# An mlp1 product of 64 rows issued inside the row-max visits (mixed attention and mlp kernel)

## The chip, the cores and the metric

The kernel runs on one core of one Trainium2 chip. The metric is the device time of one execution in microseconds; 1118.32 us is the median of 3 runs of the kernel before (1118.24 to 1118.5).

## What is computed

All inputs are float32. For 2048 tokens x of width 448, with 16 heads of 28 numbers and an mlp of width 1792:

```python
def _A_ref(x, wqkv, wo):
    qkv = transpose((x @ wqkv).reshape(B, S, 3, H, Dh), 2, 0, 3, 1, 4)
    q, k, v = qkv[0], qkv[1], qkv[2]
    scores = jnp.einsum("bhqd,bhkd->bhqk", q, k) * (Dh ** -0.5)
    p = _softmax(scores, axis=-1)
    o = jnp.einsum("bhqk,bhkd->bhqd", p, v)
    return transpose(o, 0, 2, 1, 3).reshape(B, S, D) @ wo

def _B_ref(x, w1, b1, w2, b2):
    y = _layernorm(x, axis=-1)
    h = _gelu(jnp.einsum("bsd,df->bsf", y, w1) + b1)
    return jnp.einsum("bsf,fd->bsd", h, w2) + b2

x = A_x
g = _sigmoid((x * gate_w).sum(-1, keepdims=True))
return g * _A_ref(x, A_wqkv, A_wo) + (1 - g) * _B_ref(x, B_w1, B_b1, B_w2, B_b2)
```

## The kernel before

**Precision.** Matrix products run in float32r. To come near float32 an operand is split in a high and a low part, and a product is made of three: high by high, high by low, low by high.

**Stages.** First q, k, v and the layernorm's statistics (L157 to L341); then the mlp (L599 to L668); then attention, four groups of four heads, with the output projection in the last group. In all stages TensorE (PE) has one hand-written order of instructions.

**The mlp** takes the tokens in NC = 4 groups `c` of 512. For each group, 14 calls of `mlp1(c, f)` (L564) make 128 of the 1792 hidden features each, and then four calls of `mlp2(c, i)` (L579) make 128 tokens' output each. The contraction of mlp1 is 448 = 3 x 128 + 64 long. Its first three parts take three products each. For the last 64 rows the launch code stores the weights twice, in rows 0 to 63 and 64 to 127, and `ln_low` (L140) puts the high part of y in rows 0 to 63 and the low part in rows 64 to 127 of `yh[:, 3]`. So two products of 128 rows do for them: `w1h[f][:, 3]` by `yh[:, 3]` is high by high plus high by low, and `w1l[f][:, 3]` by `yh[:, 3]` is low by high, plus low by low, which isn't needed. That makes 11 products of 128x128 weights by 512 columns in a call (L572), all added up in PSUM bank 0 or 1 (`f % 2`). Two ScalarE gelus read the bank (L575, L576). A call of mlp2 makes 42 products of 448 columns (L585, L586, L590).

**Row maxima beside it.** The softmax needs the maximum of each row of scores. `RowMax` (L343) computes, ahead of attention, scores of q by k from the high parts alone and reduces them. Its work is cut in groups `n` of 4 heads and 512 queries. In a group, 64 products of 28 contraction rows (L402) are to be made: 16 for each head `j`, whose rows lie at `32 * j`, so that head 0 has strip 0 (rows 0 to 27), head 1 strip 1 and so on. A 65th step, `close` (L366), transposes the finished maxima (L368) in the next group's time. `issue(first, n, rows)` (L374) makes `n` such products in PSUM banks `first`, `first + 1`, ...; it takes each from the head with the most left, or from the heads in `rows`, and falls back on the head with the most left if those have none. VectorE reduces the banks, two neighbouring ones in one instruction (L384) where the columns of their results ascend, and one alone otherwise (L382).

**When.** `Filler` (L426) spreads 482 of the row-max steps (MLP_MAX) evenly over the mlp stage. After each mlp1 product the code calls `filler.run` with that product's slot, 0.233 (W1; 0.65 of it in the first group of tokens), and in mlp2 with 0.205 (W2) or twice that. When at least MG = 6 steps are due, `run` makes one **visit**: `issue(2, 6)`, six steps in banks 2 to 7. The rest of the row maxima is made in the attention stage. When a group is nearly done, `issue` loads the next queries (L410), and near the end of a group of heads it has the keys of the next one loaded by `load_khr` (L460), a quarter of the keys at a time, once all four heads have used it (L413).

Of the kernel before, what the change touches and what calls it, by code (L numbers as in the profile page):

```python
# [32 lines left out]
MG = 6  # L33
FS = 4
W1, W2 = 0.233, 0.205
# [6 lines left out]
def kernel(ctx: ExitStack, tc: tile.TileContext, xt, wqk, wv, wo, xk, w1, b1, w2, b2,  # L42
                          ident_d, sel_d, out):
    nc = tc.nc
# [38 lines left out]
    w1h, w1l, w2h, w2l = {}, {}, {}, {}  # L83
# [36 lines left out]
    yh, yl = (my.tile([P, n, CH], F32R, name=f"y{n}") for n in (4, 3))  # L120
# [222 lines left out]
    class RowMax:  # L343
# [29 lines left out]

        def issue(self, first, n, rows=None):  # L374

            held = []

            def reduce():
                if held:
                    (b0, c0), (b1, c1) = held[0], held[-1]  # L380
                    if b0 == b1:
                        nc.vector.reduce_max(self.mx[:, c0:c0 + 1], bank[:, b0], axis=AX)  # L382
                    else:
                        nc.vector.reduce_max(self.mx[:, c0:c1 + 1:c1 - c0], bank[:, b0:b1 + 1], axis=AX)  # L384
                    held.clear()

            for b in range(first, first + n):
                if self.done >= NG * NC * 65:
                    break
                self.done += 1  # L390
                left = sum(len(x) for x in self.left)
                if self.last is not None and (left <= 56 or self.n == NG * NC):
                    reduce()
                    self.close(bank[:, b])
                    continue
                most = max(range(4), key=lambda j: (len(self.left[j]), -j))
                j = max(rows, key=lambda j: len(self.left[j])) if rows else most
                if not self.left[j]:
                    j = most
                i, k = self.left[j].pop(0)  # L400
                r = slice(32 * j, 32 * j + DH)
                nc.tensor.matmul(bank[:, b], self.qds[self.n][r, i * P:(i + 1) * P],  # L402
                                 khi[self.n // NC][r, k * 512:(k + 1) * 512], start=True, stop=True)
                at = (j * TPC + i) * 4 + k
                if held and held[0][1] > at:
                    reduce()
                held.append((b, at))
                if len(held) == 2:
                    reduce()
                if left == 41 and self.n + 1 < NG * NC:  # L410
                    self.load(self.n + 1)
                g, c = divmod(self.n, NC)
                if c == NC - 1 and g < MLP_G and all(n != k for x in self.left for _, n in x):  # L413
                    load_khr(g + 1, k)
                if left == 1:
                    reduce()
                    self.last = mpool.tile([P, 4 * TPC], F32, name="mf")
                    nc.vector.reduce_max(self.last, self.mx.rearrange("p (a k) -> p a k", k=4), axis=AX)
                    if self.n + 1 < NG * NC:
                        self.begin(self.n + 1)  # L420
                    else:
                        self.n += 1
                        self.left = [[]] * 4
            reduce()

    class Filler:  # L426
# [19 lines left out]
            left = self.upto - self.done  # L446
            return left if self.slot >= self.slots else min(left, int(due))

        def run(self, n=1):


            if self.max is not None and self.due(n) >= min(MG, self.upto - self.done) > 0:
                self.max.issue(2, min(MG, self.upto - self.done))

    filler = Filler()

# [3 lines left out]
    def load_khr(g, k=None, queue=nc.sync):  # L460

        sl = slice(0, S) if k is None else slice(k * CH, (k + 1) * CH)
        for j in range(4):
            r = D + (4 * g + j) * DH
            queue.dma_start(khr[32 * j:32 * j + DH, sl].bitcast(F32), qk[0, r:r + DH, sl])
# [98 lines left out]
    def mlp1(c, f):  # L564

        ps = bank[:, f % 2]
        ops = []
        for t in range(3):
            ops += [(w1h[f][:, t], yh[:, t]), (w1h[f][:, t], yl[:, t]), (w1l[f][:, t], yh[:, t])]
        ops += [(w1h[f][:, 3], yh[:, 3]), (w1l[f][:, 3], yh[:, 3])]  # L570
        for i, (a, b) in enumerate(ops):
            nc.tensor.matmul(ps, a, b, start=(i == 0), stop=(i == len(ops) - 1))  # L572
            filler.run(W1 if c else 0.65 * W1)
        h = mh.tile([P, CH], F32, name="h", bufs=2)
        nc.scalar.activation(hh[f], ps, AF.Gelu_apprx_tanh, bias=b1s[:, f:f + 1])  # L575
        nc.scalar.activation(h, ps, AF.Gelu_apprx_tanh, bias=b1s[:, f:f + 1])  # L576
        nc.gpsimd.tensor_sub(hl[f], h, hh[f].bitcast(F32))  # L577
# [21 lines left out]
    with texts:  # L599
# [12 lines left out]
        for c in range(NC):  # L612
            for f in range(NF):
                if c == 0:
                    if f == 0:
                        stages += [lnr[:, 0], lnr[:, 1]]
                        filler.max = RowMax()
                    for k in stage(f - 1):
                        low(k)
                    for k in order[3 * f // 2:3 * (f + 1) // 2]:  # L620
                        fetch_w2(k) if k < NF else fetch_w1(k - NF, staged())
                    for k in stage(f):
                        high(k)
                    if f == 1:
                        load_khr(0, queue=nc.gpsimd)
                    if f == FS:
                        filler.spread(nc.sync, MLP_MAX, 11 * W1 * (0.65 * (NF - FS) + 3 * NF) + W2 * (3 * NF * (NT - 1) - 24))
                mlp1(c, f)
            if c == 0:
                rest = order[3 * (NF - 1) // 2 - 1:]  # L630
# [5 lines left out]
            if c == NC - 1:  # L636
# [3 lines left out]
                first = {3: aq.tile([P, S], F32, name="klo", bufs=2), 2: aq.tile([P, NT, P], F32, name="vg", bufs=2)}  # L640
# [152 lines left out]
    with tc.manual_schedule(engines=ENGINES):  # L793
# [7 lines left out]
        while u < 4 * steps:  # L801
# [4 lines left out]
            while at < units[-1] // 4:  # L806
                at += 1
                n, k = divmod(at, NT)
                g, c = divmod(n, NC)
# [47 lines left out]
            if ended:  # L857
                n = summed // NT - 1
# [62 lines left out]
```

## Time and profile before

| | us |
|---|---|
| median of 3 runs | 1118.32 (1118.24 to 1118.5) |
| the profiled execution | 1119.32 |
| its span, first to last instruction | 1117.5 |
| mlp stage within it, about | 117 to 467 |
| VectorE pair reductions (L384), 203, mean of one | 1.22 |
| VectorE single reductions (L382), 618, mean of one | 0.69 |

How to read the profile: PE is TensorE's products, PEld its weight loads, which can run beside products; DVE is VectorE, ACT ScalarE, POOL GpSimd, SP the engine that issues most DMAs. A row of the timeline has the start, the length, the engine, the line of the kernel, the operation, the tiles written and read, the shapes (28*128 is 28 contraction rows by 128 weight columns) and how many instructions are merged in it; in brackets stands how long the engine was idle before, and what ended the wait. The ends of PE's products are modelled, and a product's row is longer than its share of a stream, so prices are taken from differences of starts. Row names such as `y` and `w1f` leave buffer numbers out.

### The profile page before, as it was taken

How to read it: one execution, taken by the hardware profiler on the slowest of the kernel's cores; microseconds unless marked ns; L12 is line 12 of the kernel's file. 1: busy time of each engine (PE TensorE's matmuls, PEld its weight loads, DVE VectorE, ACT ScalarE, POOL GpSimd, SP SyncE). 2: the span in 40 equal slices, each digit the busy share in tenths (PEclk: the TensorE clock that was granted, in tenths of full speed). 3: DMA queues.
4: the chain of work that ended last, by engine and by line, in shares of the span. 5: the costliest groups of instructions: out<-in, count | busy, mean ns of one | idle time of the engine just before them, and what ended most of it. 6: DMA issues, size and time to landing. Idle time of an engine off the chain costs nothing.

```text
span 1117.5 us, 19782 instructions
## 1 busy us (share of the span) xinstructions
PE 1105.8 (99%) x8136; PEld 672.7 (60%) x8136; DVE 738.9 (66%) x1029; ACT 634.4 (57%) x662; POOL 333.4 (30%) x354
## 2 busy tenths in 40 slices
PE   7999999999999999999999999999999999999998
PEld 5888777777777777744444444444444444454546
DVE  3534398988889889576766766676667767746103
ACT  5324551230241132288787877887877878847572
POOL 4006665343334331013113221320223024342350
PEclk9999999999999999999999999999999999999999
DMA  8988541011120113163100220012021003002111
GB/s 263 302 273 309 170 135 58 9 47 36 50 55 32 30 43 96 38 157 89 28 18 19 61 69 22 22 28 52 26 60 36 18 20 94 12 26 70 55 32 58
DMA packets 53079, 84.35 MB, mean 75 GB/s; under 512 B 8516, under 2 KB 28500, under 8 KB 52076
## 3 DMA queue, kind: packets, MB, share of 16 engines
q1 hardware_dynamic: 48732, 76.27, 22.7%
q0 software_dynamic: 4256, 6.81, 2.5%
q8 instruction: 64, 1.05, 0.4%
q14 instruction: 27, 0.22, 0.1%
HBM read 56.40 MB, written 26.49 MB: 74 GB/s over the span
## 4 chain that ended last, share of the span: by engine, by line
PE 96%; DMA 2%; DVE 1%; ACT 1%; POOL 0%; SPq 0%; issue 0%
PE bank L788 22%; PE bank L525 20%; PE bank L402 16%; PE bank L572 13%; PE bank L207 5%; PE bank L590 5%; PE bank L585 4%; PE bank L586 4%; PE bank L223 3%; PE bank L693 1%; PE bank L694 1%; PE bank L695 1%; DMA raw<-in_xt 1%; DMA raw<-in_wqk 1%; DMA raw<-in_wv 0%; DMA s<-in_w 0%
## 5 line engine op out<-in xcount | busy, mean ns | idle before, releaser
L529 ACT ACTIVATE pt<-bank 128x1536 f32<-128x1536 f32 (+1 forms) x387 | 461.9, 1244 | 141.0 <-PE bank L525 140.8
L382 DVE TENSOR_REDUCE mx<-bank 128x1 f32<-128x512 f32 x618 | 409.6, 687 | 173.1 <-PE bank L402 159.1
L788 PE MATMUL bank<-pt,vg 128*32 128x512 f32 x1950 | 261.6, 602 | 0.0
L384 DVE TENSOR_REDUCE mx<-bank 128x2 f32<-128x1024 f32 x203 | 238.9, 1219 | 29.2 <-PE bank L402 28.8
L402 PE MATMUL bank<-khi,qd 28*128 28x512 f32 x512 | 241.7, 479 | 0.1
L402 PEld LDWEIGHTS bank<-khi,qd 28*128 28x128 f32 x512 | 92.3, 181 | 148.1 <-DVE mx L382 106.9
L525 PE MATMUL bank<-qh,klo 28*128 28x512 f32 x1024 | 174.7, 393 | 0.0
L525 PE MATMUL bank<-qh,khi 29*128 29x512 f32 x768 | 157.2, 480 | 0.0
L572 PE MATMUL bank<-y,w1f 128*128 128x512 f32 x616 | 152.4, 398 | 1.1 <-ACT h L576 1.1
L572 PEld LDWEIGHTS bank<-y,w1f 128*128 128x128 f32 x616 | 112.5, 188 | 34.8 <-issue 10.9
L525 PE MATMUL bank<-ql,khi 28*128 28x512 f32 x768 | 129.6, 390 | 0.0
L577 POOL TENSOR_TENSOR hl<-h,hh 128x512 fp32r<-128x512 f32 x56 | 73.7, 1317 | 117.5 <-ACT h L576 77.3
L788 PEld LDWEIGHTS bank<-pt,vg 128*32 128x32 f32 x1950 | 44.6, 108 | 77.2 <-issue 76.7
L525 PEld LDWEIGHTS bank<-qh,klo 28*128 28x128 f32 x1024 | 87.6, 185 | 4.0
L575 ACT ACTIVATE hh<-bank,b1s 128x512 fp32r<-128x512 f32 x56 | 38.5, 687 | 90.3 <-PE bank L572 90.3
L709 POOL DMA_DIRECT2D lt<-ob x15 | 10.9, 725 | 250.9 <-DVE ob L708 250.9
L596 ACT ACTIVATE h<-bank 128x448 f32<-128x448 f32 x16 | 8.7, 545 | 134.5 <-PE bank L590 100.2
L590 PE MATMUL bank<-w2h,hl 128*128 128x448 f32 x224 | 85.0, 379 | 0.0
L525 PEld LDWEIGHTS bank<-qh,khi 29*128 29x128 f32 x768 | 60.8, 181 | 39.6 <-ACT pt L529 26.7
L585 PE MATMUL bank<-w2h,hh 128*128 128x448 f32 x224 | 83.3, 372 | 0.0
L586 PE MATMUL bank<-w2l,hh 128*128 128x448 f32 x224 | 81.9, 365 | 0.0
L402 PE MATMUL bank<-khr,qd 28*128 28x512 f32 x512 | 80.1, 467 | 0.2 <-DVE mx L384 0.2
(122 smaller groups left out, 1294.6 us busy)
## 6 DMA issues: line engine op xcount, KB each, us to landing
qk<-hl SPq DMA_DIRECT2D x28, 512.0 KB
raw<-in_xt SPq DMA_DIRECT2D x16, 256.0 KB
vs<-vt SPq DMA_DIRECT2D x16, 256.0 KB
s<-in_xt SPq DMA_DIRECT2D x16, 256.0 KB
rc<-rls POOLq DMA_DIRECT2D x60, 64.0 KB, 2.2
bxr<-in_xk SPq DMA_DIRECT2D x8, 448.0 KB
gbs<-h SPq DMA_DIRECT2D x16, 224.0 KB
klo<-qk SPq DMA_DIRECT2D x16, 224.0 KB
```

The lines of the kernel that those rows point to most:

```text
L207: nc.tensor.matmul(ps, a, b, start=(i == 0), stop=(i == len(ops) - 1))
L382: nc.vector.reduce_max(self.mx[:, c0:c0 + 1], bank[:, b0], axis=AX)
L384: nc.vector.reduce_max(self.mx[:, c0:c1 + 1:c1 - c0], bank[:, b0:b1 + 1], axis=AX)
L402: nc.tensor.matmul(bank[:, b], self.qds[self.n][r, i * P:(i + 1) * P], khi[self.n // NC][r, k * 512:(k + 1) * 512], start=True, stop=True)
L525: nc.tensor.matmul(bank[:, p], a[r, k * P:(k + 1) * P], b[r], start=(i == 0), stop=(i == 2))
L529: nc.scalar.activation(t, bank[:, at[0]:at[-1] + 1], AF.Exp, scale=SCALE)
L572: nc.tensor.matmul(ps, a, b, start=(i == 0), stop=(i == len(ops) - 1))
L577: nc.gpsimd.tensor_sub(hl[f], h, hh[f].bitcast(F32))
L585: nc.tensor.matmul(a, hh[f][:, sl], w2h[f], start=(f == 0), stop=False)
L586: nc.tensor.matmul(a, hh[f][:, sl], w2l[f], start=False, stop=False)
L590: nc.tensor.matmul(a, hl[f][:, sl], w2h[f], start=False, stop=(f == NF - 1))
L788: nc.tensor.matmul(pv[32 * j:32 * j + 32, :], vg[n // NC][:, k, 32 * j:32 * j + 32], probs.pop(4 * step + j), start=(k == 0), stop=(k == N ...
```

## The change

`mlp1` asks `filler.visits` whether a visit falls behind one of the first nine of the call's eleven slots. If so, the eleventh product, `w1l[f][:, 3]` by `yh[:, 3]`, is left out of the list, and its rows 0 to 63 alone (low by high, without low by low) are issued as a product of their own at the start of the first visit in the call, into the call's own bank. The six steps of that visit take their heads in a fixed order: 2, 3, 0, 1, 2, 3. The tenth product then closes the sum, and the eleventh slot is still counted. Without such a visit the call stays as it was.

```diff
@@ issue
-                j = max(rows, key=lambda j: len(self.left[j])) if rows else most
+                of = rows[b - first] if rows and isinstance(rows[0], list) else rows
+                j = max(of, key=lambda j: len(self.left[j])) if of else most
                 if not self.left[j]:
                     j = most
@@ Filler
-        def run(self, n=1):
+        def run(self, n=1, half=None):
             if self.max is not None and self.due(n) >= min(MG, self.upto - self.done) > 0:
-                self.max.issue(2, min(MG, self.upto - self.done))
+                m = min(MG, self.upto - self.done)
+                if half is None or m < MG:
+                    self.max.issue(2, m)
+                    return False
+                first, product = half
+                product()
+                side = [2, 3] if first == 0 else [0, 1]
+                self.max.issue(2, m, [[side[0]], [side[1]]] + [[j] for j in range(4)])
+                return True
+            return False
+
+        def visits(self, slots):
+            if self.max is None:
+                return 0
+            slot, done, n = self.slot, self.done, 0
+            for x in slots:
+                slot += x
+                due = self.first + (self.upto - self.first) * min(1, slot / self.slots) - done
+                if slot < self.slots and min(self.upto - done, int(due)) >= MG:
+                    done += MG
+                    n += 1
+            return n
@@ mlp1
-        for i, (a, b) in enumerate(ops):
-            nc.tensor.matmul(ps, a, b, start=(i == 0), stop=(i == len(ops) - 1))
-            filler.run(W1 if c else 0.65 * W1)
+        slot = W1 if c else 0.65 * W1
+        alone = filler.visits([slot] * 9) == 0
+        rest = lambda: nc.tensor.matmul(ps, w1l[f][:64, 3], yh[:64, 3], start=False, stop=False)
+        for i, (a, b) in enumerate(ops if alone else ops[:-1]):
+            nc.tensor.matmul(ps, a, b, start=(i == 0), stop=(i == len(ops) - (1 if alone else 2)))
+            if filler.run(slot, None if alone or rest is None else (0, rest)):
+                rest = None
+        if not alone:
+            assert rest is None
+            filler.slot += slot
```

## The prediction

> **What bounds the kernel now.** I began with the page. Its first part and its chain of waits agree on one engine:
>
> ```profile
> span 1117.5 us, 19782 instructions
> ...
> PE 1105.8 (99%) x8136; PEld 672.7 (60%) x8136; DVE 738.9 (66%) x1029; ACT 634.4 (57%) x662; POOL 333.4 (30%) x354
> ...
> PE 96%; DMA 2%; DVE 1%; ACT 1%; POOL 0%; SPq 0%; issue 0%
> ```
>
> PE is never without work, so time is gained only by giving it less. The change lies in the mlp stage, about 117 to 467 us. The busy times by stretch show it at one mlp1 phase (202 to 247) and the mlp2 phase after it:
>
> ```profile
> 202.00:247.00 45.00, 45.00 (x223) 31.85 (x223) 40.11 (x44) 16.45 (x26) 16.73 (x13) 1.00 0.14 35
> 247.00:291.00 44.00, 44.00 (x236) 34.77 (x235) 38.78 (x40) 5.09 (x9) 16.58 (x13) 1.00 0.13 40
> ```
>
> The columns after the length are PE, weight loads, DVE, ACT, POOL, the granted clock and DMA. PE is full, the clock 1.00, and DVE busy 89% (40.11 of 45.00): second in line, with little to spare. Next the timeline of PE in one piece of mlp1:
>
> ```profile
> 301.43 3.47 PE L572 MATMUL bank<-y,w1f 128*128 128x512 f32 x14
> 304.83 0.73 PE L402 MATMUL bank<-khr,qd 28*128 28x512 f32 x6
> 305.49 3.24 PE L572 MATMUL bank<-y,w1f 128*128 128x512 f32 x13
> 308.66 0.80 PE L402 MATMUL bank<-khr,qd 28*128 28x512 f32 x6
> 309.39 0.50 PE L572 MATMUL bank<-y,w1f 128*128 128x512 f32 x1
> ```
>
> Two prices come from it. **One mlp1 product**: 14 take 3.47 us and 13 take 3.24, so one more costs 0.23 us. (The 0.39 us that a row gives for one product overlaps the next.) **One visit**: from 301.43 to 305.49 are 4.06 us with 14 products, and 4.06 - 14 x 0.23 = 0.84; I take 0.86, since 0.23 is rounded up from 0.2275. The six products of a visit go four together in the four strips of 32 rows and then two, so two passes of 0.23. The other 0.40 us goes on changing from products of 128 rows to products of 28 and back: 0.20 for each change. The weight loads at the same place show what a change is:
>
> ```profile
> 304.83 0.30 PEld L402 LDWEIGHTS bank<-khr,qd 28*128 28x128 f32 x6 [0.35 <-issue]
> 305.49 2.82 PEld L572 LDWEIGHTS bank<-y,w1f 128*128 128x128 f32 x13 [0.37 <-issue]
> 308.66 0.48 PEld L402 LDWEIGHTS bank<-khr,qd 28*128 28x128 f32 x6 [0.35 <-DVE mx L384]
> ```
>
> Between products of one shape a load runs beside the product before it (13 loads in 2.82 us, no idle time listed). At a change the load starts only after PE has emptied (0.35 and 0.37 us idle), and then nothing covers it.
>
> **The change part by part.** *How often.* The filler owes 482 products over 248.5 units of slot time and calls at six: 3.09 units, or 13.3 mlp1 slots of 0.233 (20 in the first group of tokens, whose slots count 0.65). Walking the slot counter through the loops gives 81 visits, 40 inside mlp1; the same walk of the reductions gives 203 in pairs and 69 single, which the trace has:
>
> ```profile
> L384 DVE TENSOR_REDUCE mx<-bank x203: 1202/1218/1229, 132.5 to 460.1; 128x2 f32<-128x1024 f32 x102
> ...
> L382 DVE TENSOR_REDUCE mx<-bank x69: 668/682/693, 193.2 to 459.5; 128x1 f32<-128x512 f32 x69
> ```
>
> So the walk can be trusted. For the new code it gives 32 shared visits (a call in the first nine slots of eleven), in 32 of the 56 mlp1 calls.
>
> *What it removes.* 32 of these rows:
>
> ```profile
> L572 PE MATMUL bank<-y,w1f x616: 387/389/504, 117.1 to 427.0; 128*128 128x512 f32 x154
> ```
>
> 32 x 0.23 = **-7.4 us**. The low-by-low half of that product goes too, at no price, since a product's time here is that of its 512 columns.
>
> *What it adds.* 32 products of 64 rows in strips 0 and 1, each issued ahead of two visit products in strips 2 and 3, and then four more, one in each strip. If all share, a visit is still two passes (64 rows with 2 and 3; then 0, 1, 2, 3) and the whole -7.4 stays. The trace has no product of 64 rows, and never two shapes of this kind in flight together. The nearest rows are its changes of shape. 128 to 28 rows and back cost 0.20 each, above. A change of columns alone, at 128 rows, is in the last quarter, p times v to the output projection:
>
> ```profile
> 983.64 1.06 PE L788 MATMUL bank<-pt,vg 128*32 128x512 f32 x8
> 984.63 0.47 PE L693 MATMUL bank<-woh,oh 128*128 128x448 f32 x1
> ...
> 984.63 0.19 PEld L693 LDWEIGHTS bank<-woh,oh 128*128 128x128 f32 x1 [0.84 <-issue]
> ```
>
> There too the load comes after the emptying (idle 0.84). One change is free:
>
> ```profile
> 230.41 0.28 PE L368 MATMUL bank<-ident,mf 128*16 128x128 f32 x1
> 230.44 1.40 PE L572 MATMUL bank<-y,w1f 128*128 128x512 f32 x5
> ```
>
> A transpose with 16 columns is followed 0.03 us later by a full product: the number of columns used is not by itself a change. The price of 64 beside 28 rows is then between 0 (all share; less is not possible, since the two passes remain) and two changes, 0.40, with a pass of its own. I take **one change and a pass of its own**: 64 rows are a third shape, and changes of rows have always emptied PE here. In a shared visit PE then goes 128, 64, 28, 128: the pass 0.23 and the change 0.20, 32 x 0.43 = **+13.8 us**.
>
> In the Trainium skill, "TensorEngine Tiling (Array Packing)", section "Tiling Modes" (Key Properties) says that changing the tiling mode, not just the tile, drains TensorE, and lists 64-row and 32-row tiling as different modes. By that rule a 64-row product cannot run with 28-row ones and the sum is the one I take; the emptying at 304.83 agrees, but no run here has 64 rows.
>
> *What it moves.* Shared visits take two products each from strips 2 and 3 and one each from 0 and 1. A group has 16 per strip, so after some eight of them strips 2 and 3 are used up and strips 0 and 1 left: other visits then go 0, 1, 0, 1, 0, 1, three passes in place of two. The walk finds 7 more such visits: 7 x 0.23 = **+1.6 us**. Four times the strips run out inside a shared visit, and two of these need a pass more, +0.5. I set against it, as an estimate, the waits for DVE that visits have now (0.80 us at 308.66 where 304.83 has 0.73) and that a visit longer by 0.20 no longer meets: together **0**. DVE's list gets shorter: 214 pairs and 47 singles, because row order 2, 3, 0, 1, 2, 3 pairs up. DVE is hidden behind PE, and stays so while PE gets slower.
>
> *Queues.* Nothing is added to SP or POOL. The reload of the key block (L465) comes when all strips have finished a quarter, for strips 0 and 1 up to a visit or two later; it takes
>
> ```profile
> DMA to landing us min/median/max: 5.9/6.7/8.0
> ```
>
> and the next group needs a later quarter only after two or three visits, which are 3.83 us apart (304.83 and 308.66 above), so it stays covered; uncovered, it would cost one wait of a few us, once. The gelu on ACT reads a bank that is used again two calls later, about 5 us; there is no wait to lose.
>
> *Sum*: -7.4 + 13.8 + 1.6 = **+8.0 us**. The profiled execution took 1119.32 us with a span of 1117.5, so 1.8 lie outside; the change makes that span 1125.5. The median of the runs shown is 1118.32, 1.0 below the profiled one, and the forecast from it is **1126.3 us**.
>
> **The rivals.**
>
> *Strips are kept apart (1119.4, no difference).* Only products whose rows overlap wait for each other. For it: the strips need not go in step, as in the scores:
>
> ```profile
> 701.65 0.40 PE L525 MATMUL bank<-qh,klo 28*128 28x512 f32 x3
> 701.80 0.50 PE L525 MATMUL bank<-qh,khr 29*128 29x512 f32 x1
> 701.89 0.40 PE L525 MATMUL bank<-ql,khr 28*128 28x512 f32 x3
> ```
>
> One strip starts at 701.80 between three others at 701.65 and 701.89. Every emptying that the trace shows is between products that overlap in rows, so it doesn't speak against. Then the 64 rows run with strips 2 and 3, but strip 0's next product overlaps them and waits as at any change. A shared visit gains 0.23 and pays 0.20: 32 x -0.03 = -1.0; with 1.6 for the seven visits and 0.5 for the two shared ones, +1.1 us. The Trainium skill, "TensorE: Matmul & The Clock Gate", section "Part 3: Packing small matmuls — row/col tiling" (The mechanism), has weight loads overlap products in flight only when the row group differs, which is this rival's condition; no row here shows it for unlike shapes.
>
> *All share (1115.0, faster: the other side).* The change from 64 to 28 rows in the same strips is free as well. The place is the second pass of the shared visit, and the point from which it decides: the change must cost under 0.23 - (1.6 + 0.5)/32 = 0.16 us for any gain. Free, it gains 7.4, and gives back 1.6 + 0.5, and something to DVE:
>
> ```profile
> 305.36 0.69 DVE L382 TENSOR_REDUCE mx<-bank 128x1 f32<-128x512 f32 x1 [0.48 <-PE bank L402]
> 305.97 2.35 DVE L384 TENSOR_REDUCE mx<-bank 128x2 f32<-128x1024 f32 x2
> 308.23 0.68 DVE L382 TENSOR_REDUCE mx<-bank 128x1 f32<-128x512 f32 x1
> ```
>
> One visit's reductions end at 308.91, 0.25 after the next visit began at 308.66, and that visit took 0.80 instead of 0.73. With one product less between, it would begin 0.23 earlier and its last banks would hold PE by up to as much, in every second visit or so: between 0 and 32 x 0.23, and by the 20-odd visits that follow another closely about 2.0 us. -7.4 + 2.1 + 2.0 = -3.3. Against it: every change of rows in the trace costs 0.20.
>
> *The product does not go with the visit at all* is my forecast itself.
>
> **How the numbers follow.** Own pass and a change: 0.42, and 0.08 for dearer forms of it (a second change, 32 x 0.20 more, would be 1132.7). Strips apart: 0.27, and 0.02 for other sums near none. All share: 0.16, and 0.05 for more (no DVE wait: 1113.0). A measurement of this kernel can tell about 0.2%, 2.2 us, from no change; by that line faster has 0.21, within 0.29, slower 0.50. The range 1114.2 to 1128.0 takes in the three cases and leaves out the dearest and the cheapest, some 0.13. The likeliest alone: 1125 to 1128.
>
> **What would show it.** 584 full L572 products and 32 of 64 rows. Right: from the 64-row product to the first L402 after it some 0.43 us, with L402's loads idle about 0.35 before; a shared visit, from the last 128-row product to the next, 0.43 us longer than 304.83 to 305.49. Strips apart: the first two L402 start a few ns after the 64-row product, and the third about 0.43 after it. All share: that third start at about 0.33, and weight loads of L402 that wait for mx more often. Wrong altogether: another count of shared visits, or a wait on khr that isn't there now.

## The result and the profile after

The changed kernel takes 1126.93 us (median of 6 runs, 1126.38 to 1127.46), and the kernel before, run beside it, 1118.9 (6 runs, 1118.24 to 1119.44). The ratio is 1.0071, with a 95% interval of 1.006 to 1.0082: 6.7 to 9.2 us slower. The forecast was 8.0 us slower, 1126.3.

The page of the changed kernel, its first part and its chain:

```profile
span 1125.3 us, 19764 instructions
...
PE 1113.8 (99%) x8136; PEld 671.4 (60%) x8136; DVE 737.4 (66%) x1018; ACT 634.8 (56%) x662; POOL 333.3 (30%) x354
...
PE 96%; DMA 2%; DVE 1%; ACT 0%; POOL 0%; issue 0%; SPq 0%
```

The span is longer by 7.8 us and PE's busy time by 8.0, with the same number of records. PE is 96% of the chain, as before, so the time must be found on PE. Where it is, the timeline shows by the first product of each phase: here are the starts of the second group's mlp1 and of the mlp2 after it, first before, then after.

```profile
201.13 1.09 PE L572 MATMUL bank<-y,w1f 128*128 128x512 f32 x4
...
247.09 0.36 PE L585 MATMUL bank<-w2h,hh 128*128 128x448 f32 x1
```

```profile
201.93 1.09 PE L601 MATMUL bank<-y,w1f 128*128 128x512 f32 x4
...
250.21 0.37 PE L618 MATMUL bank<-w2h,hh 128*128 128x448 f32 x1
```

The phase takes 48.3 us in place of 46.0 (250.21 - 201.93 and 247.09 - 201.13), and the third and fourth groups' mlp1 give the like (48.4 for 46.1 and 47.6 for 45.9). The first group's, where four calls share, takes 40.9 us in both. The line numbers have moved: mlp1's product is L601 now (L572 before), the 64-row product L599, a visit's product L404 (L402), the reductions L385 in pairs and L383 single (L384, L382). The profile's rows for the two products (the last figures are shapes in a sample):

```profile
L599 PE MATMUL bank<-y,w1f x32: 498/498/498, 138.5 to 431.4; 64*128 64x512 f32 x32
```

```profile
L601 PE MATMUL bank<-y,w1f x584: 387/389/506, 117.6 to 434.4; 128*128 128x512 f32 x195
```

So 32 calls share, as counted. All 32 records of the 64-row product are 498 ns long, where a product in a stream has 389 ns, and the weight loads stood idle some 0.35 us before each: none had its weights loaded beside another product. One shared visit, in the timelines of PE and of the weight loads:

```profile
303.62 1.07 PE L601 MATMUL bank<-y,w1f 128*128 128x512 f32 x4
304.62 0.50 PE L599 MATMUL bank<-y,w1f 64*128 64x512 f32 x1
305.05 0.73 PE L404 MATMUL bank<-khr,qd 28*128 28x512 f32 x6
305.71 0.73 PE L601 MATMUL bank<-y,w1f 128*128 128x512 f32 x2
```

```profile
304.62 0.18 PEld L599 LDWEIGHTS bank<-y,w1f 64*128 64x128 f32 x1 [0.35 <-issue]
305.05 0.30 PEld L404 LDWEIGHTS bank<-khr,qd 28*128 28x128 f32 x6 [0.25 <-issue]
305.71 0.53 PEld L601 LDWEIGHTS bank<-y,w1f 128*128 128x128 f32 x3 [0.36 <-issue]
```

There are three emptyings in place of two. The first visit product starts 0.43 us after the 64-row one (305.05 - 304.62), although its strip is 2 and the 64 rows lie in strips 0 and 1; the same 0.43 us lies behind all 32. L404's loads were idle 0.25 us there, not the 0.35 that the prediction gave as a sign: the 64-row load takes 0.18 of the 0.43. From there the visit is the old one: six products, 0.66 us to the next full product (305.71 - 305.05, as 305.49 - 304.83 before).

### The profile page after: what moved, and what is told of

It is laid out like the page before. It is cut to its first block, busy times and chain, and to the rows that moved or that the text cites. A ratio compares the mean times of both kernels' runs of the same rounds, so it can differ in the third digit from the quotient of the medians.

```text
span 1125.3 us, 19764 instructions
## 1 busy us (share of the span) xinstructions
PE 1113.8 (99%) x8136; PEld 671.4 (60%) x8136; DVE 737.4 (66%) x1018; ACT 634.8 (56%) x662; POOL 333.3 (30%) x354
## 4 chain that ended last, share of the span: by engine, by line
PE 96%; DMA 2%; DVE 1%; ACT 0%; POOL 0%; issue 0%; SPq 0%
PE bank L821 22%; PE bank L550 20%; PE bank L404 15%; PE bank L601 12%; PE bank L207 5%; PE bank L623 5%; PE bank L618 4%; PE bank L619 4%; PE bank L223 3%; PE bank L726 1%; PE bank L599 1%; PE bank L727 1%; PE bank L728 1%; DMA raw<-in_xt 1%; DMA raw<-in_wqk 1%; DVE mx L383 0%
## 5 line engine op out<-in xcount | busy, mean ns | idle before, releaser
L383 DVE TENSOR_REDUCE mx<-bank 128x1 f32<-128x512 f32 x596 | 394.6, 688 | 171.4 <-PE bank L404 157.3
L385 DVE TENSOR_REDUCE mx<-bank 128x2 f32<-128x1024 f32 x214 | 250.7, 1220 | 40.3 <-PE bank L404 40.0
L404 PE MATMUL bank<-khi,qd 28*128 28x512 f32 x512 | 241.7, 479 | 0.1
L404 PEld LDWEIGHTS bank<-khi,qd 28*128 28x128 f32 x512 | 92.3, 181 | 148.1 <-DVE mx L383 106.9
L601 PE MATMUL bank<-y,w1f 128*128 128x512 f32 x584 | 144.9, 398 | 0.4 <-ACT h L609 0.4
L601 PEld LDWEIGHTS bank<-y,w1f 128*128 128x128 f32 x584 | 106.6, 188 | 34.4 <-issue 12.2
L821 PEld LDWEIGHTS bank<-pt,vg 128*32 128x32 f32 x1950 | 44.6, 108 | 77.2 <-issue 76.8
L404 PE MATMUL bank<-khr,qd 28*128 28x512 f32 x512 | 81.3, 462 | 0.3 <-DVE mx L385 0.2
```

The source lines that it names most:

```text
L821: nc.tensor.matmul(pv[32 * j:32 * j + 32, :], vg[n // NC][:, k, 32 * j:32 * j + 32], probs.pop(4 * step + j), start=(k == 0), stop=(k == N ...
```

## The experiments

All ratios are to the kernel before, run on the same chip in the same job. Three theories were set against each other. The height of a product is its number of contraction rows. **Height**: products of unlike height (128, 64, or the 32 of a strip) never run together, whatever their strips; a change of height empties PE. **Strips**: only products that overlap in rows wait. **Product**: it is this product that is kept apart, because it adds into an open bank, or because of the loads behind it, whatever its height.

**The product with 32 rows.** One number is changed, in both operands:

```diff
-        rest = lambda: nc.tensor.matmul(ps, w1l[f][:64, 3], yh[:64, 3], start=False, stop=False)
+        rest = lambda: nc.tensor.matmul(ps, w1l[f][:32, 3], yh[:32, 3], start=False, stop=False)
```

> The shared product takes 32 rows in place of 64 (rows 32 to 63 of low by high are left out in 32 calls). Height theory (products of unlike row height never run together, whatever their strips): 32 rows are of the same strip height as the visit's 28, so the product runs in the first pass beside strips 2 and 3; the first L404 starts a few ns after it, and the time is that of the rival in which all share, before - 3.3 us, ratio 0.997. Product theory (it is this product itself that is kept apart, because it adds into an open bank or is followed by loads that wait for VectorE): the pass of its own stays, before + 8 us, ratio 1.007. Strip theory (only overlapping rows wait) gives the same as the height theory here.

Measured: ratio 0.9976 (0.9968 to 0.9985), 2.7 us faster than before. PE's timeline in two shared visits:

```profile
202.92 0.49 PE L599 MATMUL bank<-y,w1f 32*128 32x512 f32 x1
202.93 0.73 PE L404 MATMUL bank<-khr,qd 28*128 28x512 f32 x6
203.58 2.99 PE L601 MATMUL bank<-y,w1f 128*128 128x512 f32 x12
206.50 0.49 PE L599 MATMUL bank<-y,w1f 32*128 32x512 f32 x1
206.51 1.06 PE L404 MATMUL bank<-khr,qd 28*128 28x512 f32 x6
207.50 3.24 PE L601 MATMUL bank<-y,w1f 128*128 128x512 f32 x13
```

The same product into the same open bank now starts within 0.01 us of the visit's first, in all 32 shared visits, and costs no pass. The product theory falls. The second visit shows what a free product runs into: it takes 1.06 us in place of 0.73, because its last banks are still with VectorE:

```profile
207.06 0.19 PEld L404 LDWEIGHTS bank<-khr,qd 28*128 28x128 f32 x2 [0.27 <-DVE mx L385]
```

**The product left out.**

```diff
-        rest = lambda: nc.tensor.matmul(ps, w1l[f][:64, 3], yh[:64, 3], start=False, stop=False)
+        rest = lambda: None
```

> As the changed kernel, but the 64-row product is left out altogether (low by high of the last 64 rows is missing in 32 calls): what a product that costs nothing would give. By the prediction's terms: -7.4 + 1.6 + 0.5 and 2.0 of waits for VectorE, before - 3.3 us, ratio 0.997. If VectorE has room after all: before - 5.3, ratio 0.995. If VectorE already sets the pace: before, ratio 1.000. Changed kernel less this one is the price of a 64-row product in a visit: 32 x 0.43 = 13.8 us less the waits that vanish, some 11 to 14.

Measured: 0.9975 (0.9964 to 0.9986), -2.8 us, the same as with 32 rows. So 32 rows beside a visit cost nothing that can be measured, and 64 rows cost the difference to the changed kernel, 0.0096 of 1119, 10.7 us, just under the 11 to 14 that were expected. In the profiles the later groups' mlp1 phases bear it: with 64 rows 48.27, 48.35 and 47.58 us, with the product left out 44.58, 45.05 and 44.76. The difference, 9.8 us for 28 shared calls, is 0.35 a call, less than 0.43. What is missing is put down to waits for VectorE, which the longer visits would meet less often; that was not shown apart. What the traces do show is that such waits come with the free product: in the 35 visits of these phases, loads in mid-visit were idle for VectorE 4.0 us in sum with the product left out, and 1.3 in the kernel before.

**The product last.** Heads 0, 1, 2, 3, 2, 3, and then the product, so that the second pass leaves strips 0 and 1 to it:

```diff
+                self.max.issue(2, m, [[j] for j in (0, 1, 2, 3, 2, 3)])
                 product()
-                side = [2, 3] if first == 0 else [0, 1]
-                self.max.issue(2, m, [[side[0]], [side[1]]] + [[j] for j in range(4)])
```

> The 64-row product goes last in the visit, with heads in order 0, 1, 2, 3, 2, 3, so that it could run beside strips 2 and 3 in the second pass. Height theory: again a pass of its own after an emptying, as the changed kernel, before + 8 us, ratio 1.007. Strip theory: it waits for strips 0 and 1 only, and a visit gains 0.23 and pays 0.20, before + 1.1 us, ratio 1.001.

Measured: 1.0079 (1.0065 to 1.0093). The 64-row product starts after the visit has emptied, and the full ones 0.42 us after it:

```profile
206.99 0.74 PE L404 MATMUL bank<-khr,qd 28*128 28x512 f32 x6
207.66 0.49 PE L598 MATMUL bank<-y,w1f 64*128 64x512 f32 x1
208.08 1.20 PE L600 MATMUL bank<-y,w1f 128*128 128x512 f32 x4
```

0.67 us lie between the first two starts (207.66 - 206.99), two passes and an emptying, with nothing shared. The strip theory falls in this direction too.

**A second product of 64 rows.**

```diff
-        rest = lambda: nc.tensor.matmul(ps, w1l[f][:64, 3], yh[:64, 3], start=False, stop=False)
+        def rest():
+            nc.tensor.matmul(ps, w1l[f][:64, 3], yh[:64, 3], start=False, stop=False)
+            nc.tensor.matmul(bank[:, 2], w1l[f][64:, 3], yh[64:, 3], start=True, stop=True)
```

> The changed kernel with a second 64-row product behind the first, on rows 64 to 127 (low by low, into bank 2, where the visit's first product overwrites it). Height theory: two products of one height in different strips share a pass, as the 28-row ones do: the second costs nothing, and the time is that of the changed kernel, ratio 1.007. If products of 64 rows run one at a time: 32 x 0.23 = 7.3 us more, ratio 1.0137. A wait for VectorE to free bank 2 earlier than the visit needs it isn't expected, since bank 2 is the first that it frees.

Measured: 1.0083 (1.0069 to 1.0098). That is the changed kernel within the intervals, and 1.0137 is excluded. The two run together:

```profile
205.41 0.50 PE L600 MATMUL bank<-y,w1f 64*128 64x512 f32 x1
205.42 0.49 PE L601 MATMUL bank<-y,w1f 64*128 64x512 f32 x1
205.84 0.73 PE L404 MATMUL bank<-khr,qd 28*128 28x512 f32 x6
```

Both start within 0.01 us, in strips 0, 1 and 2, 3; the 28-row products wait 0.43 us for both. Strip, place in the visit, number of products and height were varied, and the height alone decided.

**64 rows among products of 128**, in the kernel before:

```diff
-        ops += [(w1h[f][:, 3], yh[:, 3]), (w1l[f][:, 3], yh[:, 3])]
+        ops += [(w1h[f][:, 3], yh[:, 3]), (w1l[f][:64, 3], yh[:64, 3])]
```

> The kernel before, with the last product of every mlp1 call cut to 64 rows at its own place in the call, among products of 128 rows, and with no part in the visits: the price of a change of height by itself. Height theory: 56 products of 64 rows, each with a change before and a change after it of 0.20 us, less some 8 calls where a visit stands next to it and one change is had anyway: 56 x 0.40 - 8 x 0.20 = 20.8 us, ratio 1.019. If a 64-row product among 128-row ones costs nothing (the emptying in the visits is for another reason): ratio 1.000.

Measured: 1.0174 (1.0158 to 1.019), 19.5 us; with some 104 changes (2 x 56 less 8) that is 0.19 us each, against the 0.20 worked out in the prediction. The loads show both changes of one product:

```profile
206.97 1.22 PEld L572 LDWEIGHTS bank<-y,w1f 128*128 128x128 f32 x6 [0.25 <-issue]
208.56 0.18 PEld L572 LDWEIGHTS bank<-y,w1f 64*128 64x128 f32 x1 [0.36 <-issue]
208.98 1.23 PEld L572 LDWEIGHTS bank<-y,w1f 128*128 128x128 f32 x6 [0.24 <-issue]
```

Half the rows gave no gain that shows, and the two changes around a product cost some 0.4 us.

**The order of heads alone.** The full eleventh product stays, nothing goes with the visit, only the heads are taken 2, 3, 0, 1, 2, 3:

```diff
-        rest = lambda: nc.tensor.matmul(ps, w1l[f][:64, 3], yh[:64, 3], start=False, stop=False)
-        for i, (a, b) in enumerate(ops if alone else ops[:-1]):
...
+        rest = lambda: None
+        for i, (a, b) in enumerate(ops):
...
```

The rest of the edit keeps the count of slots as it was.

> The fixed order of heads 2, 3, 0, 1, 2, 3 alone: the call keeps its eleventh product of 128 rows, and no product goes with the visit. If the order costs what the prediction gave it (7 visits of three passes more, 1.6 us, and nothing in sum for the rest): before + 1.6 us, ratio 1.0014. If the order costs nothing: ratio 1.000, and the 64-row product has to answer for all of the 8 us.

Measured: 1.0015 (1.0006 to 1.0024), 1.7 us, as expected. PE's timeline of this run has visits of three passes beside the usual ones (0.96 and 0.73 us long; from start to the next full product 0.89 and 0.66):

```profile
233.34 0.96 PE L404 MATMUL bank<-khr,qd 28*128 28x512 f32 x6
234.23 3.48 PE L601 MATMUL bank<-y,w1f 128*128 128x512 f32 x14
237.64 0.73 PE L404 MATMUL bank<-khr,qd 28*128 28x512 f32 x6
```

Of the 81 visits of the mlp stage eight last 0.89 us without a wait for VectorE inside them; in the kernel before none does. The prediction's count was seven, and two more among the shared visits.

**Two products of 32 rows.** If height decides, the 64 rows should go as two products of 32. With their data where it lies, in strips 0 and 1, both would add into one bank from different strips with nothing to order them; that was not tried. Instead both quarters are brought into one strip by small copies, and run in its first and second pass, while the other three strips take two visit products each:

```diff
...
+        s = slice(32 * (f % 4), 32 * (f % 4) + 32)
+        rest = (lambda: nc.tensor.matmul(ps, w1l[f][s, 3], yq[s, 0], start=False, stop=False),
+                lambda: nc.tensor.matmul(ps, w1q[f // 4][s], yq[s, 1], start=False, stop=False))
...
+                products[0]()
+                a, b, c = (j for j in range(4) if j != strip)
+                self.max.issue(2, m, [[j] for j in (a, b, c, c, a, b)])
+                products[1]()
...
```

> All of the reference's work, with the 64 rows as two products of 32 rows in one strip, one in each pass of a shared visit, while the other three strips take two visit products each; the strip changes from call to call, so that no strip falls behind. It costs small copies (a swapped high part of y, five ACT instructions for each group of tokens, and a swapped quarter of the low weights, one small instruction for each call) and takes its room from one buffer less for raw loads and one less for the q and k results. Height theory: both are free, -7.4 us of products, about 2 back to VectorE, none for the strips: before - 5 us, ratio 0.9955, unless the buffers or copies cost something; less than the -2.7 of the run with 32 rows would be put down to these. Product theory: each quarter takes a pass, ratio above 1.005.

Measured: 1.008 (1.0065 to 1.0094), 14 us off what was expected. The row of mlp1's product says where most of it went:

```profile
L612 PE MATMUL bank<-y,w1f x584: 387/389/506, 127.5 to 438.5; 128*128 128x512 f32 x195
```

The first mlp1 product comes at 127.5 us, not at 117.1: the first stage, with two buffers fewer, is 10 us longer. (The profiled execution took 1131.0 us, 3 more than the median.) The loss is whole in the first 60 us: PE made 180 products there, 228 in the kernel before. The later groups' mlp1 took 45.93, 45.73 and 45.36 us against 45.96, 46.08 and 45.91, a gain of only 0.9. The same kernel with the slot W1 counted 0.218:

> As the one before, with the slot of an mlp1 product counted 0.218 in place of 0.233, so that the visits are spread by the time that the calls now take: fewer visits in mlp1 and more in mlp2. If VectorE's lag inside mlp1 holds back some 2 us: up to 1 us faster than the one before, ratio 0.9945. If the number of shared visits is what counts: 1 to 2 fewer a group of tokens, each 0.23 us, some 1 us slower than the one before, ratio 0.9965.

Measured: 1.0076 (1.0063 to 1.0089). It can't be told from the run before it by the ratio. Its mlp1 phases were shorter than there, 44.8, 44.8 and 44.6 us, its mlp2 phases some 1.2 longer in sum. Then the room was taken after the first stage, the swapped weights were made by ScalarE behind the first group of tokens, and that group was left as it was. The first lines stand against the two runs above:

```diff
-    yq = my.tile([P, 2, CH], F32R, name="yq")
+    yq = mh.tile([P, 2, CH], F32R, name="yq")
...
+        alone = c == 0 or filler.visits([slot] * 9) == 0
```

> All of the reference's work, two products of 32 rows in one strip as before, but no buffer of the first stage is given up: the room for the swapped parts is taken after it, and the first group of tokens keeps its eleven products, so 28 calls share. If the 10 us by which the first mlp1 product came late in the earlier run with quarters (127.5 after 117.1) were the missing buffers, the stage starts at 117 again. Its mlp1 phases of the later groups took 45.9, 45.7 and 45.4 us against 46.0, 46.0 and 45.9: before - 1 us, ratio 0.999. If the copies on ACT cost the start: ratio above 1.003.

Measured: 0.9999 (0.9991 to 1.0008). The stage starts on time again. The copies moved together with the buffers, so the buffers as the cause are likely and not shown apart: in the first 60 us of the run that started late POOL and ACT were no busier than before (13.7 and 24.9 us; before 13.7 and 26.1).

```profile
L614 PE MATMUL bank<-y,w1f x588: 387/389/506, 117.4 to 426.4; 128*128 128x512 f32 x196
```

28 products of 0.23 are gone (616 - 588), 6.4 us, and the time is that of before within 1 us. The gain is given back inside the visits: the 35 of these three phases take 30.9 us in sum, where the kernel before has 25.2. Part of it is waits for VectorE (3.3 us of idle loads in mid-visit, 1.3 before). Another part is third passes: six visits last 0.89 to 1.13 us with no such wait, none does before. One of them:

```profile
221.67 0.49 PE L611 MATMUL bank<-yq,w1f 32*128 32x512 f32 x1
221.68 0.51 PE L407 MATMUL bank<-khr,qd 28*128 28x512 f32 x3
222.00 0.42 PE L612 MATMUL bank<-yq,w1q 32*128 32x512 f32 x1
222.02 0.64 PE L407 MATMUL bank<-khr,qd 28*128 28x512 f32 x3
222.59 3.02 PE L614 MATMUL bank<-y,w1f 128*128 128x512 f32 x12
```

It lasts 0.92 us (222.59 - 221.67), a pass more than usual; the code gives a visit product another strip when its own has none left. And with W1 = 0.218:

> The same with the slot of an mlp1 product counted 0.218: the mlp1 phases with it took 44.8, 44.8 and 44.6 us in the earlier run, 3.7 less than before, and the mlp2 phases about 1.2 more: before - 2.5 us, ratio 0.998. If the gain of fewer visits in mlp1 is all given back in mlp2: ratio 0.999, as the one beside it.

Measured: 0.9966 (0.9954 to 0.9979). Fewer visits fall in mlp1 with this slot, so 25 calls share in place of 28. The same kernel on another chip:

> The quarters with slot 0.218 once more, on the same chip as the slot alone, so that the two can be set against each other: ratio 0.9966 again.

Measured: 0.9977 (0.9968 to 0.9986). So 2.6 to 3.8 us faster than the kernel before, with the reference's whole work. A visit of it:

```profile
204.79 0.50 PE L611 MATMUL bank<-yq,w1f 32*128 32x512 f32 x1
204.79 0.72 PE L407 MATMUL bank<-khr,qd 28*128 28x512 f32 x4
205.13 0.38 PE L612 MATMUL bank<-yq,w1q 32*128 32x512 f32 x1
205.14 0.39 PE L407 MATMUL bank<-khr,qd 28*128 28x512 f32 x2
205.46 3.23 PE L614 MATMUL bank<-y,w1f 128*128 128x512 f32 x13
```

Eight products take 0.67 us (205.46 - 204.79), where six took 0.66 before. Is it the quarters, or the slot alone? The kernel before with nothing but the slot:

> The kernel before with nothing but the slot of an mlp1 product counted 0.218 in place of 0.233: how much of the gain of the quarters with that slot (ratio 0.9966) is the spread of the visits alone. If the quarters are what gains: the kernel before waits for VectorE hardly at all (9.6 us of idle loads put down to mx in its later groups, most of it the emptying that a change has anyway), so ratio 0.9995 to 1.000. If the spread alone gains: 0.997.

Measured: 0.9996 (0.9988 to 1.0005). The slot by itself gives nothing that can be measured, and the quarters with the old slot give nothing either (0.9999): the gain takes both.

## Why the prediction was right

- **What is removed**: 32 full products, 7.4 us by 0.23 each. The counts are those of the walk (x584, x32).
- **A pass of its own and one change more, 0.43 us a shared visit**: 0.43 in the timeline after. This was the disputed term. The prediction took it because every change of rows in the trace emptied PE, and said that no row had products of unlike height in different strips. So it was a bet, with a chance of 0.42, that the price of a change between overlapping rows holds for strips that don't overlap. The runs with 32 rows, with the product last and with two of 64 settled it. The rule of the Trainium skill named there ("TensorEngine Tiling (Array Packing)", section "Tiling Modes", Key Properties) holds for heights here, also where no rows overlap. The Trainium skill, "TensorE: Matmul & The Clock Gate", section "Part 3: Packing small matmuls — row/col tiling" (The mechanism), has weight loads overlap products in flight only when the row group differs. Here different strips were not enough: 64 and 28 rows started 0.43 us apart (304.62 and 305.05), and two of 64 rows within 0.01 (205.41 and 205.42).
- **Seven visits of three passes, 1.6 us**: 1.7 us, 0.7 to 2.7 by the interval, by the order alone.
- **Two more passes and the waits for VectorE set to 0 together**: not measured apart. -7.4 + 13.8 + 1.6 is 8.0 and the ratio gives 7.9, but its interval of 6.7 to 9.2 leaves these two together some 1.3 us either way. That the sum comes within 0.1 us is partly luck: the four shared calls of the first group, counted at 0.20 each, don't show in its mlp1 phase. VectorE did get less to do, as said: its pair reductions rose and its single ones fell over the whole kernel, by the walk's 11 and 22:

```profile
L383 DVE TENSOR_REDUCE mx<-bank 128x1 f32<-128x512 f32 x596 | 394.6, 688 | 171.4 <-PE bank L404 157.3
L385 DVE TENSOR_REDUCE mx<-bank 128x2 f32<-128x1024 f32 x214 | 250.7, 1220 | 40.3 <-PE bank L404 40.0
```

- **The rival in which all share** was priced at -3.3 us, 2.0 of them given back to VectorE. A product that costs nothing gave -2.8 (-4.0 to -1.6): the price was right within the interval, the condition (64 beside 28 rows) did not hold.
- **What was missed** came in the experiments: -5 us for the quarters was off, first by the longer first stage (10 us in its trace), then because with the old slot the visits took back 5.6 of 6.4 us. That expectation had given about 2 us back to VectorE and nothing to the strips.

Open: whether two products of 32 rows in different strips can add into one bank, and how the 5.6 us that the quarters' visits take back divide exactly between waits for VectorE and third passes; both are seen, and they were not varied apart.

## What to carry to other kernels

In these runs products ran together on TensorE only if they had the same height (28, 29 and 32 rows count as one), so cut a remainder to the height of the products that it is to go with (32 beside 28), not to what it happens to need (64). A product with fewer rows was no cheaper by itself: 56 products of 64 rows in place of 128 made the kernel 19.5 us slower, since each change of height around them costs about 0.2 us. Before a gap on the bound engine is filled, look at the second engine and at the order of the work: with VectorE busy 89%, its waits and third passes took back most of what the quarters gave until the visits were spread anew.

## What the runs showed of the hardware

A change of height costs about 0.2 us in each pair measured, with or without overlapping rows: 0.20 for 128 to 28 and for 28 to 128 (a visit's 0.86 us less two passes, shared by two changes), 0.19 for 128 to 64 and for 64 to 128 (19.5 us for 104 changes), 0.20 for 64 to 28 (0.43 less a pass of 0.23). Two 64-row products in different halves start within 0.01 us and cost one pass (ratio 1.0083 against 1.0071 with one). A product with 32 contraction rows and products with 28 count as one height: they start within 0.01 us, and the kernel takes as long as without the 32-row product (0.9976 and 0.9975).
